# Three real products for a complex mix, an exact softshrink, and row swaps by SBUF transfers, in a Fourier mixer fused with a feed-forward block

## The chip, the cores and the metric

One core of a Trainium2 chip runs the whole program. The metric is the device time of one execution in microseconds (us); runs of one kernel mostly agree within 0.3%, and a kernel counts as faster or slower when its ratio to the one before differs from 1 by over 2%. Engines: TensorE (PE; its weight loads are PEld), VectorE (DVE), ScalarE (ACT), GpSimd (POOL), and SyncE (SP), which issues most transfers.

## The reference, cut to what matters

```python
# attention part: x is (8, 3008, 256)
X = np.fft.rfft(x, axis=1);  Xr, Xi = X.real, X.imag
Yr = Xr @ w_r - Xi @ w_i + b_r
Yi = Xr @ w_i + Xi @ w_r + b_i
Y  = softshrink(Yr, 0.01) + 1j * softshrink(Yi, 0.01)   # sign(y) * max(|y| - 0.01, 0)
y  = np.fft.irfft(Y, n=3008, axis=1)
# feed-forward part on the 24064 rows of y
h = np.maximum(y @ w_in, 0);  out = (s * h * h + b) @ w_out    # 256 -> 2048 -> 256
```

The feed-forward part is most of the arithmetic. The Fourier transform of length 3008 = 94 x 32 is done as matrix products: a first DFT over 94, a second over 32 (with twiddles), the complex mix with w_r and w_i, the inverse over 32, and the last DFT over 94.

## The kernel before: the parts concerned

The program interleaves two streams on TensorE. "Tiles" of the feed-forward block are cut in slots (one slot: two matmuls of the first layer and four or so of the second). Into chosen slots it puts small "units" of the transform of later batches: the second DFT, mix and inverse of batch b run while the feed-forward block works on batch b-1. Batch 0 has its own code at the start.

```python
def fwd_unit(i):                     # second DFT, two row groups
    ...                              # 4 matmuls -> one PSUM bank
    xt = xfpool.tile([P, 2 * DC, 192], F16)
    evac(xt[:, :, 64:192], ps, 512)                     # ACT or DVE, by a load balance
    nc.vector.tensor_scalar_mul(out=xt[:, :, 0:64], in0=xt[:, :, 128:192], scalar1=-1.0)

def mix_unit(i):                     # Xr w_r - Xi w_i and Xr w_i + Xi w_r
    for j in range(2):
        for m, (w, lo) in enumerate(((0, 64), (1, 0))):
            for dc in range(DC):
                matmul(ps[:, j, :], xt[:, j * DC + dc, lo : lo + P], W_t[:, dc, w], ...)   # 8 in all
    nc.vector.tensor_tensor(out=m, in0=ps, in1=lamb, op=max)
    nc.vector.scalar_tensor_tensor(out=z, in0=ps, scalar=2 * LAM, in1=m, op0=add, op1=min)

def inv_unit(i): ...                 # 2 matmuls with z, one copy to v, stored to DRAM
def s4_unit(g):                      # last DFT
    nc.vector.scalar_tensor_tensor(out=yt[...], in0=off, scalar=bl, in1=ps, op0=mult, op1=add)
```

The two DVE ops of the mix give the softshrink up to a constant offset, and the last DFT takes the offset's transform off again. All units share two PSUM banks (`psf`). In the views, `psh` and `psa` are the PSUM tiles of the feed-forward block's two layers, `rt` and `gt` its SBUF tiles; `u` goes to DRAM as `ud` and comes back as `us`, and `v` likewise. Line numbers (L557) differ from kernel to kernel.

## Time and profile before

| | before |
|---|---|
| time, median (4 runs) | 884.32 us (884.15 to 887.18) |
| span in the profile | 881.7 us, mean granted TensorE clock 0.999 |
| busy: PE, DVE, ACT, POOL | 97%, 75%, 71%, 3% |
| mix | 672 matmuls of 256 columns |
| transfers by the SP queue | 76,802 packets, 70 MB, 26.8% of the 16 engines' span |

The prediction below shows the lines and how they are read. The point to keep is that a matmul's listed duration is its depth in the pipe; the start-to-start distance is the pace.

### The profile page before, as it was taken

The numbers are of one execution on the slowest core, as the hardware profiler recorded it, in microseconds if no ns is written. First come the engines' busy times: TensorE is split into PE (matmuls) and PEld (weight loads), VectorE is DVE, ScalarE is ACT, GpSimd is POOL, SyncE is SP. The second block draws the span as 40 slices with busy tenths as digits, with TensorE's granted clock in tenths as the row PEclk, the third lists the DMA queues.
The fourth block names the chain that finished last, engine by engine and source line by source line (L and its number), as shares of the span: only waits on it lengthen the run. The fifth ranks groups of instructions, "written<-read, shape, count | busy, mean of one in ns | idle before, by whom it ended". The sixth has DMA issues, their size and how long they took to land.

```text
span 881.7 us, 16393 instructions
## 1 busy us (share of the span) xinstructions
PE 856.1 (97%) x6748; PEld 613.9 (70%) x6748; DVE 659.5 (75%) x846; ACT 621.9 (71%) x779; POOL 27.7 (3%) x51
## 2 busy tenths in 40 slices
PE   4989999999999999999999999999999999999997
PEld 3856776777767766777667776777767777766665
DVE  6797778677787778777787777787777767876663
ACT  4786776766777776777777777777767776676663
POOL 4010000000000000000000000000000000000000
PEclk9999999999999999999999999999999999999999
DMA  8764156313462237412563236712254111411111
GB/s 176 131 188 123 57 123 170 116 48 73 128 176 87 60 96 177 134 49 64 135 160 95 62 83 145 185 48 61 61 161 115 48 50 49 125 37 36 36 38 54
DMA packets 83021, 87.29 MB, mean 99 GB/s; under 512 B 5502, under 2 KB 75266, under 8 KB 81474
## 3 DMA queue, kind: packets, MB, share of 16 engines
q1 hardware_dynamic: 76802, 70.25, 26.8%
q0 software_dynamic: 6144, 15.99, 10.6%
q8 instruction: 53, 0.87, 0.4%
q14 instruction: 22, 0.18, 0.1%
HBM read 53.98 MB, written 46.66 MB: 114 GB/s over the span
## 4 chain that ended last, share of the span: by engine, by line
PE 83%; DVE 5%; ACT 5%; DMA 4%; issue 2%; SPq 0%; POOL 0%; DVEq 0%; ACTq 0%; POOLq 0%
PE psa L750 33%; PE psh L681 33%; PE psf L557 8%; PE psf L507 2%; PE psf L623 2%; ACT rt L688 2%; PE psf L539 2%; PE psf L575 2%; DVE gt L695 2%; DMA x<-in_x_dram 1%; DMA vs<-vd 1%; DMA ud<-u 1%; ACT u L172 1%; DVE g L376 1%; DVE yt L628 0%
## 5 line engine op out<-in xcount | busy, mean ns | idle before, releaser
L688 ACT ACTIVATE rt<-psh 128x1024 f32<-128x1024 f32 (+2 forms) x384 | 386.3, 1007 | 175.5 <-PE psh L681 174.2
L695 DVE TENSOR_TENSOR gt<-rt 128x1024 f16<-128x1024 f32 (+2 forms) x300 | 361.8, 1208 | 136.3 <-ACT rt L688 133.3
L750 PE MATMUL psa<-w_out_t,gt 128*128 128x256 f16 (+1 forms) x3024 | 457.1, 272 | 0.1
L750 PEld LDWEIGHTS <-gt 128*128 128x128 f16 (+1 forms) x3024 | 300.1, 101 | 181.6 <-issue 1.4
L681 PE MATMUL psh<-yt,w_in 128*128 128x512 f16 (+1 forms) x1344 | 397.9, 378 | 0.0
L681 PEld LDWEIGHTS <-w_in 128*128 128x128 f16 x1536 | 144.6, 98 | 25.1 <-issue 1.2
L760 DVE SCALAR_TENSOR_TENSOR ost<-psa,s_bc,bias_bc 128x512 f32<-128x512 f32 (+1 forms) x96 | 70.9, 739 | 23.5 <-PE psa L750 21.1
L557 PE MATMUL psf<-W_t,xf 128*128 128x256 f16 x672 | 87.1, 273 | 0.3 <-DVE xf L176 0.3
L692 ACT ACTIVATE gt<-rt 128x1024 f16<-128x1024 f32 (+2 forms) x84 | 85.7, 1020 | 2.0
L557 PEld LDWEIGHTS <-xf 128*128 128x128 f16 x672 | 65.7, 98 | 8.2 <-issue 0.7
L172 ACT CAST u<-psf 96x512 f16<-96x512 f32 x93 | 53.9, 581 | 23.5 <-PE psf L507 23.5
L628 DVE SCALAR_TENSOR_TENSOR yt<-off,bl,psf 128x480 f16<-128x480 f32 (+1 forms) x98 | 61.9, 666 | 7.6 <-PE psf L623 6.5
L565 DVE SCALAR_TENSOR_TENSOR z<-psf,m 128x512 f16<-128x512 f32 x84 | 58.1, 692 | 2.9
L563 DVE TENSOR_TENSOR m<-psf,lamb 128x512 f32<-128x512 f32 x84 | 57.5, 685 | 2.7 <-PE psf L557 2.5
L172 ACT CAST v<-psf 128x512 f16<-128x512 f32 x82 | 47.6, 580 | 17.0 <-PE psf L575 17.0
L172 ACT CAST xf<-psf 128x512 f16<-128x512 f32 x79 | 46.1, 584 | 10.5 <-PE psf L539 10.5
L681 PE MATMUL psh<-tail,w_in 128*128 128x512 f16 (+1 forms) x192 | 53.4, 353 | 0.0
L507 PE MATMUL psf<-x,A_t 94*96 94x512 f16 x104 | 39.9, 383 | 1.4 <-DVE z L565 0.5
L623 PEld LDWEIGHTS <-vs 96*128 96x128 f16 x448 | 28.9, 97 | 10.3 <-issue 4.1
L623 PE MATMUL psf<-C_t,vs 96*128 96x96 f16 x448 | 33.6, 205 | 0.8 <-ACT u L172 0.3
L539 PE MATMUL psf<-F_t,us 128*128 128x128 f16 x336 | 32.5, 219 | 1.5 <-DMA us<-ud 1.3
L196 POOL DMA_DIRECT2D x<-in_x_dram x32 | 17.0, 533 | 499.8 <-PE psf L507 464.6
(73 smaller groups left out, 312.5 us busy)
## 6 DMA issues: line engine op xcount, KB each, us to landing
out_dram<-ost SPq DMA_DIRECT2D x152, 128.0 KB
x<-in_x_dram POOLq DMA_DIRECT2D x32, 376.0 KB, 6.6
ud<-u SPq DMA_DIRECT2D x28, 384.0 KB
us<-ud SPq DMA_DIRECT2D x28, 384.0 KB
vd<-v SPq DMA_DIRECT2D x42, 256.0 KB
vs<-vd SPq DMA_DIRECT2D x14, 768.0 KB
out_dram<-ost SPq DMA_DIRECT2D x16, 120.0 KB
off<-offset_signal POOLq DMA_DIRECT2D x1, 1536.0 KB, 9.7
```

The source lines that it names most:

```text
L172: return None, nc.scalar.copy(out=dst, in_=src)
L507: nc.tensor.matmul(ps[0:96, :], A_t[0:N1, :], x16[(b, c)][0:N1, j * D : (j + 2) * D], start=True, stop=True,)
L557: nc.tensor.matmul(ps[:, j, :], xt[:, j * DC + dc, lo : lo + P], W_t[:, dc, w], start=(m == 0 and dc == 0), stop=(m == 1 and dc == DC - 1),)
L565: nc.vector.scalar_tensor_tensor(out=z, in0=ps, scalar=2 * LAM, in1=m, op0=ALU.add, op1=ALU.min)
L623: nc.tensor.matmul(ps[:, j * 96 : (j + 1) * 96], vs[(b, h)][:, k, ec * P : (ec + 1) * P], C_t, start=True, stop=True,)
L628: nc.vector.scalar_tensor_tensor(out=yt[:, ec, n2 : n2 + w, :], in0=off[0][:, n2 : n2 + w, :], scalar=bl[:, 1, ec : ec + 1], in1=ps[:, 0 : ...
L681: nc.tensor.matmul(o, w_in_t[dc][:, mc * P : (mc + 1) * P], r, start=(dc == 0), stop=(dc == DC - 1),)
L688: nc.scalar.activation(out=rt[:, :, 0:w], in_=ps[:, :, 0:w], func=AF.Relu)
L692: nc.scalar.activation(out=gt[:, :, 0:w], in_=rt[:, :, 0:w], func=AF.Square)
L695: nc.vector.tensor_tensor(out=gt[:, :, 0:w], in0=rt[:, :, 0:w], in1=rt[:, :, 0:w], op=ALU.mult)
L750: nc.tensor.matmul(ps[0:size, h, :], gts[(ti, mc // 2)][:, mc % 2, sub * size : (sub + 1) * size], w_out_t[:, mc, :], start=(mc == 0), sto ...
L760: nc.vector.scalar_tensor_tensor(out=ost[0:size, 0:k], in0=ps[0:size, 0:k], scalar=s_bc[0:size], in1=bias_bc[0:size, 0:k], op0=ALU.mult, o ...
```

## The change

Its intent: with S = (Xr + Xi) w_r, one has Yr = S - Xi (w_i + w_r) and Yi = S + Xr (w_i - w_r), so three real products do the work of four. The softshrink becomes exact (y - clamp(y, -0.01, 0.01)), done on fp16 sums in SBUF, so the offset at the last DFT goes. The price is a layout: results come out with two row groups and two parts (real, imaginary) crossed, and four 32 KB SBUF to SBUF transfers per unit (the swaps) put the rows where the inverse DFT wants them. The tiles `t`, `m` and `z` of the mix lie in one SBUF buffer, called `ring` in the views, so a swap is `ring<-ring`.

```diff
 def fwd_unit(i):
-    evac(xt[:, :, 64:192], ...)
-    nc.vector.tensor_scalar_mul(out=xt[:, :, 0:64], in0=xt[:, :, 128:192], scalar1=-1.0)
+    evac(xt[:, 1:3], bank, 512)
+    nc.vector.tensor_tensor(out=xt[:, 0], in0=xt[:, 1], in1=xt[:, 2], op=ALU.add)   # Xr + Xi
+def sum_unit(h):                              # one for two mix units: 4 matmuls
+    ... matmul(ps[:, i, :], xf[2 * h + i][:, 0, dc], W_t[:, dc, 0], ...)
+    nc.scalar.copy(out=s, in_=ps)
 def mix_unit(i):
-    ... 8 matmuls; max; add-and-min from PSUM
+    ... 4 matmuls with W_g
+    nc.vector.tensor_tensor(out=t, in0=ps, in1=s, op=ALU.add)       # PSUM -> fp16 ring
+    nc.vector.tensor_tensor(out=m, in0=t, in1=low, op=ALU.max)
+    nc.vector.tensor_tensor(out=m, in0=m, in1=high, op=ALU.min)
+    nc.vector.tensor_tensor(out=t, in0=t, in1=m, op=ALU.subtract)
+    for j in range(2):
+        for r in range(2):
+            nc.sync.dma_start(out=z[64*r : 64*r+64, j], in_=t[64*j : 64*j+64, r])
...
+    # inverse units follow their mix by four units; two empty units before the last four
 def s4_unit(g):
-    nc.vector.scalar_tensor_tensor(out=yt[...], in0=off, scalar=bl, in1=ps, ...)
+    evac(yt[...], ps, w * 96)                                       # ACT or DVE
...
+    make_w_g(); make_bounds()      # five POOL ops while batch 0 is mixed
```

More of the change, by code (lines that the diff above doesn't have):

```diff
@@ L70, in _tables @@
     return first, fwd, inv, last
-def _offset_signal(inv, last):
-    v = inv.reshape(2, 2, N2, NPAIR, 2, N2).sum(axis=2)
-    v = v.transpose(0, 2, 1, 3, 4).reshape(2, 96, N2)
-    return np.einsum("rkn,km->rnm", v, last)
 def _tile_order(nb):
@@ L130 @@
     T_d = nc.inline_tensor(inv.astype(np.float16), name="dft_inv").ap()
-    off_r, off_i = _offset_signal(inv, last)
-    IMPULSE = float(off_r[0, 0])
-    off_r[0, 0] = 0.0
-    assert np.abs(off_r[:, :N1]).max() < 1e-9
-    G_d = nc.inline_tensor(off_i.astype(np.float32).reshape(1, -1), name="offset_signal").ap()
     C_d = nc.inline_tensor(last.astype(np.float16), name="dft_last").ap()
@@ L152 @@
     uspool = ctx.enter_context(tc.tile_pool(name="usp", bufs=5))
-    xfpool = ctx.enter_context(tc.tile_pool(name="xfp", bufs=3))
+    xfpool = ctx.enter_context(tc.tile_pool(name="xfp", bufs=4))
     mpool = ctx.enter_context(tc.tile_pool(name="mp", bufs=2))
-    zpool = ctx.enter_context(tc.tile_pool(name="zp", bufs=3))
     vpool = ctx.enter_context(tc.tile_pool(name="vp", bufs=3))
@@ L232 @@
     nc.sync.dma_start(out=C_t, in_=C_d)
-    b_one = cpool.tile([P, D], F32, name="b_one")
+    b_st = rpool.tile([P, 2, D], F32, name="b_st", tag="rt")
     for i, bv in enumerate((b_r, b_i)):
-        nc.sync.dma_start(
-            out=b_one[64 * i : 64 * i + 64], in_=bv.unsqueeze(0).to_broadcast([64, D])
-        )
-    lamb = cpool.tile([P, 2, D], F32, name="lamb")
-    bl = cpool.tile([P, 2, DC], F32, name="bl")
-    for i, bv in enumerate((b_r, b_i)):
-        nc.sync.dma_start(out=bl[:, i], in_=bv.rearrange("(c p) -> p c", p=P))
+        nc.sync.dma_start(out=b_st[:, i], in_=bv.unsqueeze(0).to_broadcast([P, D]))
+    low = cpool.tile([P, 2, D], F16, name="low")
+    high = cpool.tile([P, 2, D], F16, name="high")
+    W_g = cpool.tile([P, DC, 2, D], F16, name="W_g")
     s_bc = cpool.tile([P, 1], F32, name="s_bc")
@@ L270, with make_bounds, make_w_g @@
         nc.vector.memset(f, 0.0)
-    def make_lamb():
-        for j in range(2):
-            nc.vector.tensor_scalar(
-                out=lamb[:, j], in0=b_one, scalar1=-1.0, scalar2=LAM, op0=ALU.mult, op1=ALU.add
-            )
+    def make_bounds():
+        for t, c in ((low, -LAM), (high, LAM)):
+            nc.gpsimd.tensor_scalar(
+                out=t, in0=b_st, scalar1=-1.0, scalar2=c, op0=ALU.mult, op1=ALU.add
+            )
+    def make_w_g():
+        nc.gpsimd.tensor_tensor(out=W_g[:, :, 1], in0=w_st[1], in1=w_st[0], op=ALU.subtract)
+        nc.gpsimd.tensor_tensor(out=W_g[:, :, 0], in0=w_st[1], in1=w_st[0], op=ALU.add)
+        nc.gpsimd.tensor_scalar_mul(out=W_g[:, :, 0], in0=W_g[:, :, 0], scalar1=-1.0)
     def blocks(t):
@@ L315 @@
     vs = {}
+    ring = []
     yts = {}
@@ L402, in fwd_dft @@
             nc.scalar.activation(out=pos, in_=ps, func=AF.Relu, bias=neg_lam)
-            z = zpool.tile([P, 4, P], F16, name="z", tag="z")
+            z = gpool.tile([P, 4, P], F16, name="z", tag="gt")
             nc.vector.scalar_tensor_tensor(
@@ L480, in first_batch @@
             if i == 6:
-                with tc.issue_after(g_last[0].ins):
-                    make_lamb()
-                nc.gpsimd.tensor_scalar_add(out=bl[:, 1], in0=bl[:, 1], scalar1=-LAM)
-                nc.gpsimd.tensor_scalar(
-                    out=bl[:, 0], in0=bl[:, 0], scalar1=-LAM, scalar2=IMPULSE,
-                    op0=ALU.add, op1=ALU.mult,
-                )
+                make_w_g()
+                make_bounds()
         for k in range(4):
@@ L528, in s23_units @@
         vd = dpool.tile([NPAIR, P, D], F16, name="vd", tag="vd")
+        if not ring:
+            ring.append(bigpool.tile([P, 12, 2, D], F16, name="ring", tag="corr"))
         xf = {}
@@ L533, in fwd_unit @@
         def fwd_unit(i):
-            ps = one_bank().rearrange("p (j c k) -> p j c k", j=2, c=DC)
+            bank = one_bank()
+            ps = bank.rearrange("p (r c j k) -> p r c j k", r=2, c=DC, j=2)
             t = us[(b, i // 3)]
@@ L539, in fwd_unit @@
                     nc.tensor.matmul(
-                        ps[:, j, dc, :], t[:, q, dc * P : (dc + 1) * P],
+                        ps[:, :, dc, j, :], t[:, q, dc * P : (dc + 1) * P],
                         F_t[:, 2 * i + j, :], start=True, stop=True,
                     )
-            xt = xfpool.tile([P, 2 * DC, 192], F16, name="xf", tag="xf")
-            evac(xt[:, :, 64:192], ps.rearrange("p j c k -> p (j c) k"), 512)
-            nc.vector.tensor_scalar_mul(
-                out=xt[:, :, 0:64], in0=xt[:, :, 128:192], scalar1=-1.0
-            )
@@ L548, in fwd_unit @@
-            load["dve"] += 0.2
-            xf[i] = xt
-        def mix_unit(i):
-            ps = one_bank().rearrange("p (j e) -> p j e", j=2)
-            xt = xf.pop(i)
-            for j in range(2):
-                for m, (w, lo) in enumerate(((0, 64), (1, 0))):
-                    for dc in range(DC):
-                        nc.tensor.matmul(
-                            ps[:, j, :], xt[:, j * DC + dc, lo : lo + P], W_t[:, dc, w],
-                            start=(m == 0 and dc == 0), stop=(m == 1 and dc == DC - 1),
-                        )
-            m = mpool.tile([P, 2, D], F32, name="m", tag="m")
-            nc.vector.tensor_tensor(out=m, in0=ps, in1=lamb, op=ALU.max)
-            z = zpool.tile([P, 2, D], F16, name="z", tag="z")
-            nc.vector.scalar_tensor_tensor(
-                out=z, in0=ps, scalar=2 * LAM, in1=m, op0=ALU.add, op1=ALU.min
-            )
-            load["dve"] += 1.38
+            xt = xfpool.tile([P, 3, DC, P], F16, name="xf", tag="xf")
@@ new lines, in fwd_unit @@
+            evac(xt[:, 1:3].rearrange("p r c k -> p (r c k)"), bank, 512)
+            nc.vector.tensor_tensor(out=xt[:, 0], in0=xt[:, 1], in1=xt[:, 2], op=ALU.add)
+            load["dve"] += 0.25
+            xf[i] = xt
+        def sum_unit(h):
+            ps = one_bank().rearrange("p (i e) -> p i e", i=2)
+            for i in range(2):
+                for dc in range(DC):
+                    nc.tensor.matmul(
+                        ps[:, i, :], xf[2 * h + i][:, 0, dc], W_t[:, dc, 0],
+                        start=(dc == 0), stop=(dc == DC - 1),
+                    )
+            s = mpool.tile([P, 2, D], F32, name="s", tag="m")
+            nc.scalar.copy(out=s, in_=ps)
+            load["act"] += 0.6
+            hold[h] = s
@@ new lines, in mix_unit @@
+        def mix_unit(i):
+            ps = one_bank().rearrange("p (r e) -> p r e", r=2)
+            xt = xf.pop(i)
+            for r in range(2):
+                for dc in range(DC):
+                    nc.tensor.matmul(
+                        ps[:, r, :], xt[:, 2 - r, dc], W_g[:, dc, r],
+                        start=(dc == 0), stop=(dc == DC - 1),
+                    )
+            t, m = ring[0][:, i % 4], ring[0][:, 4 + i % 2]
+            nc.vector.tensor_tensor(
+                out=t, in0=ps, in1=hold[i // 2][:, i % 2].unsqueeze(1).to_broadcast([P, 2, D]),
+                op=ALU.add,
+            )
+            nc.vector.tensor_tensor(out=m, in0=t, in1=low, op=ALU.max)
+            nc.vector.tensor_tensor(out=m, in0=m, in1=high, op=ALU.min)
+            nc.vector.tensor_tensor(out=t, in0=t, in1=m, op=ALU.subtract)
+            load["dve"] += 1.75
+            z = ring[0][:, 6 + i % 6]
+            for j in range(2):
+                for r in range(2):
+                    nc.sync.dma_start(
+                        out=z[64 * r : 64 * r + 64, j], in_=t[64 * j : 64 * j + 64, r]
+                    )
@@ L597, in s23_units, with put @@
         units = []
-        for i in range(H + 2):
-            if i < H:
-                units.append(lambda i=i: fwd_unit(i))
-            if 0 <= i - 1 < H:
-                units.append(lambda i=i: mix_unit(i - 1))
-            if 0 <= i - 2 < H:
-                units.append(lambda i=i: inv_unit(i - 2))
+        def put(f, i, n):
+            if 0 <= i < n:
+                units.append(lambda: f(i))
+        for h in range(H // 2 + 3):
+            for i in range(2):
+                put(fwd_unit, 2 * h + i, H)
+                put(mix_unit, 2 * h - 2 + i, H)
+                put(inv_unit, 2 * h - 6 + i, H)
+            put(sum_unit, h, H // 2)
+            if h == H // 2:
+                units += [lambda: None] * 2
         return units
@@ L627, in unit @@
                 )
-            nc.vector.scalar_tensor_tensor(
-                out=yt[:, ec, n2 : n2 + w, :], in0=off[0][:, n2 : n2 + w, :],
-                scalar=bl[:, 1, ec : ec + 1],
-                in1=ps[:, 0 : w * 96].rearrange("p (j n) -> p j n", n=96),
-                op0=ALU.mult, op1=ALU.add,
-            )
-            load["dve"] += 0.15 + w / 10.0
-            if n2 == 0:
-                nc.vector.tensor_scalar_add(
-                    out=yt[:, ec, 0, 0:1], in0=yt[:, ec, 0, 0:1], scalar1=bl[:, 0, ec : ec + 1]
-                )
+            evac(
+                yt[:, ec, n2 : n2 + w, :],
+                ps[:, 0 : w * 96].rearrange("p (j n) -> p j n", n=96), w * 96,
+            )
             if g == len(groups) - 1 and b >= 2:
@@ L778 @@
     load.update(act=0.0, dve=0.0)
-    off = []
-    def emit_load_off():
-        off.append(bigpool.tile([P, N2, 96], F32, name="off", tag="corr"))
-        nc.gpsimd.dma_start(
-            out=off[0].rearrange("p n m -> p (n m)"), in_=G_d.to_broadcast([P, N2 * 96])
-        )
     mark = {}
@@ L793 @@
     plan.setdefault(17, []).append(lambda: emit_load_x(2))
-    plan.setdefault(30, []).append(emit_load_off)
     schedule(22, 44, s23_units(1))
```

## The prediction

> **What bounds the kernel now.** I read the page's busy table first, then its slices, then the time-ordered view of one stretch, then the waits and windows.
>
> ```profile
> PE 856.1 (97%) x6748; PEld 613.9 (70%) x6748; DVE 659.5 (75%) x846; ACT 621.9 (71%) x779; POOL 27.7 (3%) x51
> ...
> PE   4989999999999999999999999999999999999997
> ```
>
> TensorE is busy from the second slice to the last; VectorE (DVE) and ScalarE (ACT) have about a quarter free. But matmuls are pipelined, so "busy" may hide slack. The test is the pace, from the time-ordered view around 181 us:
>
> ```profile
> 181.56 1.04 PE L557 MATMUL psf<-W_t,xf 128*128 128x256 f16 x8
> 181.56 0.22 DVE L545 TENSOR_SCALAR xf<-xf 128x256 f16<-128x256 f16 x1
> 182.33 0.21 PEld L681 LDWEIGHTS <-w_in 128*128 128x128 f16 x2
> 182.38 1.23 DVE L695 TENSOR_TENSOR gt<-rt 128x1024 f16<-128x1024 f32 x1 [0.60 <-ACT rt L688]
> 182.43 0.59 PE L681 MATMUL psh<-yt,w_in 128*128 128x512 f16 x2
> ```
>
> The reader is to see the two PE starts: eight mix matmuls begin at 181.56 and the next matmul at 182.43, so eight take 0.87 us, 109 ns each, though the group row gives each a duration of 273 ns (its depth in the pipe). 256 columns at the page's full clock cannot go much faster. The windows view says that this holds all through the steady part:
>
> ```profile
> 165.00:205.00 40.00, 40.00 (x313) 29.99 (x312) 28.95 (x39) 28.52 (x36) 0.00 (x0) 1.00 0.16 47
> ```
>
> Columns: PE, weight loads, DVE, ACT and POOL busy in 40 us. PE never pauses; DVE is at 72%, ACT at 71%. The waits view charges PE only a few tenths of a us here and there after 64 us. The chain of work that ended last is 83% PE. So the bound is the stream of matmul columns; only about 15 us at the start and 12 us after the last first-layer matmul are anything else.
>
> **What the Trainium skill says.** "TensorE: Matmul & The Clock Gate", Back-to-back issue gap: 262 cycles for N=256 warm, which is 109 ns; the trace's 0.87/8 agrees exactly. "Perfetto Trace Analysis", Identifying the Most-Contended Engine, says matmul busy share is a poor measure and weight-load busy share a better one; here that share is only 70% while the pace is at its floor, so for this mix of shapes I trust the pace. "VectorE: DVE Perf Modes", The perf-mode tier table with the errata section: a two-input op runs 1x with fp32 or PSUM and 2x with 16-bit SBUF operands, and a fp32 one takes (N+151)/0.96 ns. The trace agrees for 1x: L695 with N=1024 has 1223 ns against 1224. No two-input 16-bit op is in this trace, so the 2x cost is an estimate from that page. "DMA: Bandwidth & Descriptors", Anatomy of one DMA: about 2 us fixed for a transfer, mostly the confirmation that it landed. No small SBUF copy is in this trace; the nearest thing is a 3.2 us us<-ud step in the chain of waits.
>
> **The change part by part.** The rows concerned:
>
> ```profile
> L557 PE MATMUL psf<-W_t,xf 128*128 128x256 f16 x672 | 87.1, 273 | 0.3 <-DVE xf L176 0.3
> L565 DVE SCALAR_TENSOR_TENSOR z<-psf,m 128x512 f16<-128x512 f32 x84 | 58.1, 692 | 2.9
> L563 DVE TENSOR_TENSOR m<-psf,lamb 128x512 f32<-128x512 f32 x84 | 57.5, 685 | 2.7 <-PE psf L557 2.5
> L628 DVE SCALAR_TENSOR_TENSOR yt<-off,bl,psf 128x480 f16<-128x480 f32 x84 | 56.3, 708 | 4.1 <-PE psf L623 3.2
> L545 DVE TENSOR_SCALAR xf<-xf 128x256 f16<-128x256 f16 x84 | 18.4, 222 | 17.6 <-ACT xf L172 17.4
> ```
>
> *TensorE.* Eight mix matmuls per unit become four, plus four for each two units: 672 go to 336 + 168 = 504. 168 fewer at 109 ns is **18.3 us**. Every one lies on the path that sets the end, so with nothing else changed 884.2 - 18.3 = 865.9 us, 2.1% less. All other matmuls keep their shape; the built program's instruction list confirms the counts.
>
> *VectorE.* Per mix unit, before: 0.222 + 0.685 + 0.692 = 1.60 us, times 84 = 134 us. After: the sum of two halves, 256 fp16 (estimate (128+151)/0.96 = 0.29 us); the add from PSUM (0.685, like L563); max, min and subtract on 512 fp16 (estimate (256+151)/0.96 = 0.42 each). That is 2.25 us, times 84 = 189 us: +55 us. The last-DFT evacuations lose the offset term: 62 us at L628 and 3 us of one-column fixes leave; by the built order 31 of the 98 plain copies stay on DVE (about 19 us), 67 go to ACT. The kernel's load balancer also moves 22 squares (23 us) and some 18 copies (12 us) to DVE. Sum: 659.5 + 55 - 65 + 19 + 23 + 12 = **704 us**, 81% of 866.
>
> *ScalarE.* 42 new copies of the shared product (0.58 us each, like the other L172 rows: 24 us), 67 copies from the last DFT (35 us), less 22 squares (20 us) and 18 copies (10 us): **651 us**, 75%.
>
> *Transfers.* 336 row swaps of 64 x 512 B, 32 KB each, 11 MB in all; one 1.5 MB offset load goes. The DMA share is 0.16 in the window above, so bandwidth is ample. The SP queue that issues them spends 0.37 us on a vd<-v issue and 0.57 on an output row block, so four swaps are an estimated 1.5 to 2.4 us of SP time per mix unit, which comes every 5 to 6 us. A swapped tile is now an input of the inverse DFT, but that is emitted four mix units later, some 15 to 20 us, against about 2 us of DVE chain, 2 us of issue and 2 to 3 us of landing: hidden. Only the last two units of a batch have shorter leads, about 8 us. The reshaped forward output (two runs of 64 columns) costs no columns.
>
> *Start.* The bounds and the combined weights are made on POOL while the first batch runs; POOL is 3% busy. Neutral within a us.
>
> **The rivals.** (1) *The saving is whole*: PE is at its floor and everything new hides, 866 us. For it: DVE and ACT stay under saturation on average, and 15 gt buffers let DVE lag. Against it: averages. (2) *DVE becomes the near-bound in the mix stretches.* Mix units fill only 44 to 66 of each 80 to 96 first-layer slots. Placing the durations above by slot in the built order, DVE work rises from about 0.77 to 0.89-0.97 of PE's own time there (0.98 in the densest, batch 1's 44 slots), ACT from 0.77 to 0.87; some of that is overlap between neighbours, so call it 0.85-0.94. All small matmul groups share two PSUM banks; a bank waits for its evacuation behind a 2 us DVE chain or a 1.2 us square, while units follow every 1.2 to 1.7 us. That makes short PE stalls: I put 0.05 to 0.15 us per mix unit, 4 to 12 us over 84, most in batch 1 and batch 3. Working for it: PSUM is freed after one DVE op (0.69 us) instead of two (1.38). Time 870 to 878. (3) *The swaps take the place of the removed matmuls as a wait*: SP issues in order and reuses its completion slots, so a slow 768 KB load or an output waiting for its producer would hold swaps back, and PE with them. Each batch's last units could lose 1 us: 873 or so; a lead that is too short everywhere would cost a us per unit, 950, but the four-unit lag speaks against it. (4) *Relief for the last-DFT stretch*, where DVE was fullest: worth nothing, since PE had no gaps there.
>
> **Range and chances.** 865.9 plus about 6 us of stalls: **872 us**. Low end 865 (no stalls, a us off the start), high end 884 (DVE stalls of 18 us, the gain gone). Faster by over 2% needs 866.8 or less, that is under 1 us of new stalls: 0.14. Slower by over 2% needs 36 us of stalls: 0.06. Within 2%: 0.80.
>
> **What would show it.** PE rows for the mix: 504 matmuls, 109 ns apart. DVE near 700 us, its fp16 rows near 0.42 us, 0.29 for the sum. In the windows of the mix stretches, PE short of the full stretch by a few per cent, its waits naming the ring add, the xf sum or an ACT copy (rival 2), or the ring's DMA (rival 3). It would be wrong if the 16-bit ops run at 1x (0.69 us each: +67 us of DVE, saturated, no gain or a loss), if the swaps land later than 10 us, or if PE shows no new waits at all (then 866).

## More of the kernel before

The next batch's x comes in four pieces of 376 KB, issued from POOL; each piece is fetched as soon as the first DFT has consumed the piece whose buffer it takes.

## The result

The changed kernel took 874.86 us (median of 4 runs, 873.02 to 878.13) against 884.32: ratio 0.989 with a 95% interval of 0.9852 to 0.9927. Ratios here are the mean time of one kernel's runs over that of the other's runs of the same rounds, so not quite the ratio of the medians. By the 2% rule it is "same": 1.1% faster, where the matmul count alone promised 2.1%. Its runs spread more, and with the clock: 873.0 and 873.9 us had a mean granted clock of 0.994, 875.8 and 878.1 had 0.989.

The page of the changed kernel, in the same places as the lines of before: the busy table, the PE slices, and the groups of the new mix (count, then busy us and mean ns, then idle time of the engine ahead of the group and what ended it).

```profile
PE 838.8 (96%) x6580; PEld 599.4 (69%) x6580; DVE 693.4 (80%) x971; ACT 640.7 (74%) x848; POOL 32.8 (4%) x53
...
PE   4889999999899999999999999999999999999996
...
L563 DVE TENSOR_TENSOR ring<-psf,s 128x512 f16<-128x512 f32 x84 | 57.4, 683 | 3.4 <-PE psf L558 3.3
...
L558 PE MATMUL psf<-W_g,xf 128*128 128x256 f16 x336 | 50.4, 273 | 0.0
...
L585 PE MATMUL psf<-ring,T_t 128*128 128x256 f16 x168 | 33.2, 275 | 7.7 <-DMA ring<-ring 7.6
L569 DVE TENSOR_TENSOR ring<-ring,high 128x512 f16<-128x512 f16 x84 | 35.5, 422 | 2.1
L570 DVE TENSOR_TENSOR ring<-ring 128x512 f16<-128x512 f16 x84 | 35.4, 422 | 2.0
```

The new DVE ops cost what was estimated (422 ns), DVE is 34 us busier, and one figure has no counterpart before: L585, the inverse DFT, kept PE idle for 7.6 us, waiting for the ring's transfers. The windows view says where PE still runs without a gap and where not (same columns as in the prediction; the last three are granted clock, share of the transfer engines, GB/s):

```profile
165.00:205.00 40.00, 40.00 (x313) 29.99 (x312) 33.83 (x58) 31.38 (x41) 0.00 (x0) 1.00 0.24 68
...
225.00:245.00 20.00, 16.80 (x104) 10.93 (x103) 11.88 (x15) 11.72 (x16) 0.51 (x1) 0.91 0.62 152
```

In the middle of a batch's mixes DVE is busy 85% of the time and PE 100%. At the end of the batch PE loses 3.2 us of 20, DVE is less busy than elsewhere (59%), the transfer engines are at 62%, and the clock is 0.91. The kernel before had the transfer engines as full in the same 20 us (0.61), but no swap to wait for:

```profile
225.00:245.00 20.00, 19.95 (x139) 13.79 (x137) 14.58 (x17) 14.43 (x20) 1.03 (x2) 1.00 0.61 149
```

In the changed kernel the chain of waits, in time order, names the link:

```profile
227.65 0.45 PE psh L689 x2
228.10 0.05 SPq L576
228.15 0.05 issue
228.20 7.72 DMA ring<-ring
235.92 0.14 issue
236.05 0.27 PE psf L585
```

A 32 KB swap issued at 228.2 lands at 235.9. The time-ordered view around it:

```profile
227.62 3.34 SPq L576 DMA_DIRECT2D ring<-ring  x4
...
227.95 0.51 POOL L182 DMA_DIRECT2D x<-in_x_dram  x1 [12.75 <-PE psf L493]
...
236.05 0.63 PE L585 MATMUL psf<-ring,T_t 128*128 128x256 f16 x2 [3.18 <-DMA ring<-ring]
236.48 1.06 PE L689 MATMUL psh<-yt,w_in 128*128 128x512 f16 x2
237.33 1.06 PE L758 MATMUL psa<-w_out_t,gt 128*128 128x256 f16 x4
```

Two things stand here. A piece of the next x was issued at 227.95, between the swaps. In the trace's packet records its 94 packets of 4 KB, which began between 230.0 and 235.1, held their engines for 482 ns each on the mean (median 324), where the 512-byte packets of these 9 us, the swaps' among them, took 29 ns. And after the pause PE is slow: two matmuls of 512 columns from 236.48 to 237.33 are 0.85 us, 426 ns each, in place of 216. The clock records show a stretch of 3.41 us at half clock from 236.4; another begins at 127.2, after a wait of 2.1 us that ends at 126.4. All the PE waits for the ring (2.1, 3.2, 1.2, 0.3 and 0.8 us at the ends of batches 1 to 5) have an x piece issued 1 to 8 us ahead; batches 6 and 7, which have no further x to load at that point, have none.

The start differs as well. In the time-ordered view, VectorE's four copies into `T_t`, before and after:

```profile
19.17 2.27 DVE L301 COPY T_t<-T_c 32x1536 f16<-32x1536 f16 x4
```

```profile
18.47 4.65 DVE L291 COPY T_t<-T_c 32x1536 f16<-32x1536 f16 x4
...
20.33 1.49 POOL L265 TENSOR_TENSOR W_g<-w_st 128x512 f16<-128x512 f32 x1
21.81 0.90 POOL L257 TENSOR_SCALAR low<-b_st 128x512 f16<-128x512 f32 x1
22.69 1.78 POOL L266 TENSOR_SCALAR W_g<-W_g 128x512 f16<-128x512 f16 x1
```

They take twice as long beside the new POOL ops, and the waits view of the changed kernel has a PE wait of 2.2 us for the first DVE result `g` there.

So the theory is: the saving on PE is whole; it is reduced by (A) swaps at the end of a batch that land late because a piece of x uses the same transfer engines (A1), the two longest pauses followed by half clock, and (C) POOL and DVE blocking each other at the start. The rivals: the lead of the last swaps is too short in any case (A2), or DVE at 80% is what costs (B).

### The profile page after: what moved, and what is told of

Its sections match the earlier page's. It is cut to its first block, busy times and chain, and to the rows that moved or that the text cites. A ratio compares the mean times of both kernels' runs of the same rounds, so it can differ in the third digit from the quotient of the medians.

```text
span 871.1 us, 16955 instructions
## 1 busy us (share of the span) xinstructions
PE 838.8 (96%) x6580; PEld 599.4 (69%) x6580; DVE 693.4 (80%) x971; ACT 640.7 (74%) x848; POOL 32.8 (4%) x53
## 4 chain that ended last, share of the span: by engine, by line
PE 89%; DMA 5%; ACT 2%; DVE 2%; issue 1%; SPq 1%; POOL 0%; DVEq 0%; POOLq 0%
PE psh L689 36%; PE psa L758 36%; PE psf L558 4%; DMA ring<-ring 3%; PE psf L493 3%; PE psf L529 2%; PE psf L544 2%; PE psf L638 2%; PE psf L585 2%; DMA x<-in_x_dram 1%; ACT rt L696 1%; DVE T_t L291 1%; PE psh L357 1%; ACT yt L158 0%; ACT m L393 0%
## 5 line engine op out<-in xcount | busy, mean ns | idle before, releaser
L703 DVE TENSOR_TENSOR gt<-rt 128x1024 f16<-128x1024 f32 (+2 forms) x322 | 385.8, 1200 | 111.2 <-ACT rt L696 110.7
L700 ACT ACTIVATE gt<-rt 128x1024 f16<-128x1024 f32 (+2 forms) x62 | 65.4, 1055 | 0.9
L563 DVE TENSOR_TENSOR ring<-psf,s 128x512 f16<-128x512 f32 x84 | 57.4, 683 | 3.4 <-PE psf L558 3.3
L558 PE MATMUL psf<-W_g,xf 128*128 128x256 f16 x336 | 50.4, 273 | 0.0
L158 ACT CAST yt<-psf 128x480 f16<-128x480 f32 (+2 forms) x71 | 36.4, 526 | 10.8 <-PE psf L638 10.7
L585 PE MATMUL psf<-ring,T_t 128*128 128x256 f16 x168 | 33.2, 275 | 7.7 <-DMA ring<-ring 7.6
L569 DVE TENSOR_TENSOR ring<-ring,high 128x512 f16<-128x512 f16 x84 | 35.5, 422 | 2.1
L570 DVE TENSOR_TENSOR ring<-ring 128x512 f16<-128x512 f16 x84 | 35.4, 422 | 2.0
L568 DVE TENSOR_TENSOR ring<-ring,low 128x512 f16<-128x512 f16 x84 | 35.3, 420 | 1.5
L558 PEld LDWEIGHTS <-xf 128*128 128x128 f16 x336 | 32.9, 98 | 3.7
L182 POOL DMA_DIRECT2D x<-in_x_dram x32 | 16.7, 525 | 492.3 <-PE psf L493 456.0
```

The source lines that it names most:

```text
L158: return None, nc.scalar.copy(out=dst, in_=src)
L558: nc.tensor.matmul(ps[:, r, :], xt[:, 2 - r, dc], W_g[:, dc, r], start=(dc == 0), stop=(dc == DC - 1),)
L563: nc.vector.tensor_tensor(out=t, in0=ps, in1=hold[i // 2][:, i % 2].unsqueeze(1).to_broadcast([P, 2, D]), op=ALU.add,)
L569: nc.vector.tensor_tensor(out=m, in0=m, in1=high, op=ALU.min)
L585: nc.tensor.matmul(ps[:, j, :], T_t[:, 2 * i + j, :], z[:, j, :], start=True, stop=True)
L700: nc.scalar.activation(out=gt[:, :, 0:w], in_=rt[:, :, 0:w], func=AF.Square)
```

## The experiments

Runs of one call share a chip and its runs of the kernel before (883.68, 883.83, 884.01 and 884.15 us in the four calls). Differences in us are taken from the ratios, times 884.

**1. The changed kernel again**, as the base on this chip.

> The changed kernel again, as the base for the runs beside it. Its first four runs spread from 873.0 to 878.1 us with granted clocks of 0.994 and 0.989. All theories: 873 to 878, ratio to before about 0.989. If pauses of TensorE that halve its clock are the cause of the spread, its slower runs have the lower mean clock (about 0.002 for each half-clock stretch of 3.4 us).

873.0 us (869.0 to 875.5), ratio 0.9877 (0.9856 to 0.9898), clocks 0.992 to 0.995; its slowest runs do not have the lowest clocks here, so the tie of spread and clock is loose. Its trace has the same waits at the same places (8.0 us for the ring) and half-clock stretches at 52.6, 127.7 and 236.9 us.

**2. No swaps** (wrong result).

```diff
-nc.vector.tensor_tensor(out=t, in0=t, in1=m, op=ALU.subtract)
+nc.vector.tensor_tensor(out=z, in0=t, in1=m, op=ALU.subtract)     # z = ring[0][:, 6 + i % 6]
-... four nc.sync.dma_start(...) per unit
```

> The last op of the softshrink writes straight into the inverse DFT's input and the 336 row swaps are gone (wrong result on purpose; DVE, ACT and PE work unchanged). Theory A (the lost part of the gain is PE waiting for the last swaps of a batch, and the half clock that follows): 7.6 us of waits and about 3 us of half clock go, less what takes their place: 864 to 867, clock 0.998. Rival B (VectorE as near-bound): no change, 873 to 878.

862.45 us, ratio 0.9754 (0.9741 to 0.9767): 10.9 us less than the base, a little more than theory A asked for. DVE did the same work (695 us busy), so rival B falls for this part. The forecast clock of 0.998 did not come: the runs had 0.993 to 0.997, and the profile has 6.8 us of half clock from 23.7 us, at the start, around a PE wait of 4.1 us for the first `g`. After the start it has none.

**3. The loads of x held back** past the swaps of the batch.

```diff
+def gated_load_x(b):
+    gate = nc.gpsimd.tensor_copy(out=gate_t[0:1, 0:1], in_=newest[0][0:1, 0, 0:1])  # newest gt tile
+    with tc.issue_after(gate.ins):
+        emit_load_x(b)
-plan.setdefault(s1 + 6, []).append(lambda b=b: emit_load_x(b + 1))
+plan.setdefault(s1 + 6, []).append(lambda b=b: gated_load_x(b + 1))
```

> Same kernel, but the loads of the next batch's x (376 KB pieces) are held back on POOL until six first-layer slots into the next batch, so that none runs beside the last swaps of a batch. Theory A1 (the swaps land late because a piece of x shares the transfer engines: all six PE waits come within 1 to 8 us of an x issue): waits of L585 for the ring nearly vanish, 865 to 868. Rival A2 (the lead is too short anyway, or SP issues too slowly): little change, 871 to 877. Rival B: no change.

863.68 us, ratio 0.9771 (0.9758 to 0.9783), correct: 9.4 us less than the base and a little below A1's forecast, with every swap still there. In the time-ordered view of POOL, the pieces that had come one by one now come together, well ahead of the batch's end:

```profile
167.45 0.18 POOL L679 COPY gate_t<-gt 1x1 f16<-1x1 f16 x1 [103.27 <-DVE gt L710]
167.94 2.05 POOL L182 DMA_DIRECT2D x<-in_x_dram  x4 [0.30 <-PE psf L558]
```

and of PE's waits for the ring one is left, in batch 3, with its landing in the chain of waits:

```profile
318.94 0.12 SPq L576
319.06 0.05 issue
319.11 1.83 DMA ring<-ring
320.94 0.05 issue
320.99 0.28 PE psf L585
```

A swap lands in 1.8 us where no piece of x runs beside it. The changed kernel says the same by itself: in its chain of waits, the two swaps with no piece of x issued in the 8 us before land in 2.0 us (at 115.8) and 1.8 us (at 314.1), the five others in 4.4 to 7.7. So A1 is shown: not the swap's own cost, but what it met.

**4. More lead** (rival A2).

```diff
-units += [lambda: None] * 2
+units += [lambda: None] * 6
```

> Six empty units in place of two ahead of the last four inverse DFTs of a batch, in the same span: 3 to 6 us more lead for the last swaps, the other units packed a little closer. Theory A (late swaps): 866 to 870. Rival B (VectorE): the denser packing makes it worse, 876 to 882.

874.37 us, ratio 0.9898 (0.9881 to 0.9914): no gain, so theory A's forecast for this run was wrong. The trace shows part of why. Lead did grow in batches 2 and 4 to 7 (from 5 to 9 us between the last softshrink's end and its inverse DFT to 11.5 to 12), and the waits of batches 2, 4 and 5 went. But in batch 1, which has 44 slots for now 48 units, DVE finished the last softshrink 5.2 us after its matmuls began, the swaps were issued at 125.0 behind other entries of the SP queue, a piece of x at 124.6 ran beside them, and one landed after 6.4 us: PE waited 3.5 us there, more than before, with a half-clock stretch after it. This profile also had a longer wait at the start (4.4 us against 2.2) and 6.8 us of half clock there. PE's waits for the ring still fell in sum, from 7.6 to 4.2 us. That the closer packing spent what the lead gained is argued from batch 1 alone and not shown. Nor does the run speak for rival A2, because the edit also moved the swaps relative to the loads. In batches 2, 4 and 5 the last softshrink now ended 7.0 to 7.4 us ahead of the next piece of x (1.2 to 1.6 in the changed kernel), and the waits went; in batches 1 and 3 it ended 2.0 and 3.8 us ahead, and a wait stayed.

**5. The POOL ops held back** until the `T_t` copies are done.

```diff
+gate2 = nc.gpsimd.tensor_copy(out=w_gate[96:97, 0:1], in_=T_t[96:97, 0, 64:65])
+with tc.issue_after(gate2.ins):
     make_w_g(); make_bounds()
```

> The changed kernel with one edit: the five POOL ops that make the combined weights and the bounds wait until VectorE's copies into T_t are done. In the traces of the changed kernel these copies (three in 1.7 us before) take 4.1 us beside the POOL ops, and TensorE then waits 2.2 to 4.4 us for the first DVE g. Theory C (POOL and DVE block each other there, and in some runs a half-clock stretch follows): PE's wait for the first g falls under 0.5 us and the time by 2 to 5 us, to 868 to 871. Rival (harmless, or other transfers are the cause): 871 to 875.

870.23 us, ratio 0.9842 (0.9821 to 0.9863): 3.1 us less than the base, give or take 2.6 by the two intervals; experiment 6 against 3 gives 3.3, give or take 1.7. Theory C's gain holds, and the copies are back at their old cost:

```profile
18.91 2.25 DVE L292 COPY T_t<-T_c 32x1536 f16<-32x1536 f16 x4
```

Which POOL work slowed them is less clear. The second copy of the changed kernel (19.03 to 20.70) ran mostly beside the issue of a load of w_out (19.14 to 20.33), before the first POOL op shown above, and in this run that issue came at 17.1. The edit moved both and does not separate them.

**6. Both edits.**

> Both edits, the held-back loads of x and the held-back POOL ops. If the two losses are independent they add: 863.7 less 2 to 5, so 859 to 862, mean clock 0.998 as before. If the POOL effect is nothing: 863.7.

860.57 us, ratio 0.9734 (0.972 to 0.9749), correct, and the fastest valid version here: the two gains add (9.4 + 3.1 from 0.9877 would be 0.9736). Three of its four runs have the clock 0.998 of the kernel before.

**7. Only the matmuls gone, in the kernel before** (wrong result): two of each unit's eight left out.

```diff
-for dc in range(DC):
+for dc in range(DC - m):
```

> The kernel BEFORE with two of each unit's eight mix matmuls left out (168 in all; wrong result on purpose), nothing else changed. It measures what the removed matmuls alone are worth. Theory (TensorE's pace is the bound): 168 x 109 ns = 18.3 us, so 865 to 866. Rival (part is lost to new waits on DVE even with no added DVE work): 868 to 875.

866.25 us, ratio 0.9793 (0.9775 to 0.9811): 18.3 us (16.7 to 19.9), the sum of 168 x 109 ns.

**8. The matmuls put back, in the version with both edits** (wrong result): the shared product's four matmuls twice.

```diff
-for dc in range(DC):
+for k in range(2 * DC):
+    dc = k % DC
```

> The version with both edits, with the shared product's four matmuls done twice (168 more, back to 672; wrong result on purpose). Theory (TensorE's pace is the bound after as well): both-edits time plus 18.3 us, 877 to 880. If VectorE or the transfers were the bound after the change: less, plus 5 to 12.

877.7 us, ratio 0.9924 (0.9906 to 0.9941): 16.8 us more than without them. PE's pace is the bound after the change as before it. The 1.5 us short of 18.3 are within the two intervals.

**9. Less DVE work, in the version with both edits** (wrong softshrink; the comparison still passed, so its tolerance does not tell the two apart).

```diff
-tensor_tensor(out=m, in0=t, in1=low, op=max); tensor_tensor(out=m, in0=m, in1=high, op=min)
-tensor_tensor(out=t, in0=t, in1=m, op=subtract)
+tensor_tensor(out=t, in0=t, in1=low, op=subtract)
```

> The version with both edits, with max, min and subtract of the softshrink replaced by one subtract (wrong result on purpose): 168 VectorE ops of 0.42 us fewer, 71 us of its 694, and the swaps start 0.9 us earlier. If VectorE's load (prediction's main rival, 4 to 12 us of stalls) still costs TensorE anything, the time falls from 860.6 by 3 us or more. If VectorE is hidden: within 1 us, 859.6 to 861.5.

859.01 us, ratio 0.9709 (0.9695 to 0.9722), 2.2 us less by the ratios: between the two forecasts. The windows view of the middle of a batch, for the version with both edits and for this one:

```profile
165.00:205.00 40.00, 40.00 (x313) 29.57 (x311) 34.65 (x59) 31.69 (x43) 1.22 (x3) 1.00 0.48 111
```

```profile
165.00:205.00 40.00, 40.00 (x314) 29.70 (x313) 28.52 (x44) 31.14 (x41) 1.77 (x4) 1.00 0.48 107
```

DVE fell from 87% to 71% of these 40 us and PE was full in both. PE's distance from its floor, summed over start-to-start times, differs in the middle of the program only in batch 3 (2.5 us against 1.0 between 260 and 345 us), where the last wait for a swap has gone. So these DVE ops cost about 2 us in all, and the 1.5 us of it that the trace shows went into the start of that swap, not into evacuations.

**10 and 11. What else the change gained, and a control.** The version with both edits is 5.2 us faster than experiment 7 (0.9734 against 0.9793), with the same matmul count. In the kernel before, PE's weight loads (PEld) had small waits, of which these are the largest after the start, in the waits view from 64 us on (us in total, times, longest; "issue" means that the profile shows nothing that was waited for):

```profile
PEld L623 <- issue: 4.1, 16, 0.3
PEld L507 <- DVE z L565: 3.3, 6, 0.7
```

L623 is the last DFT, L507 the first DFT behind a mix. Experiment 10 gives the kernel before the change's plain evacuation of the last DFT:

```diff
-nc.vector.scalar_tensor_tensor(out=yt[...], in0=off, scalar=bl, in1=ps, op0=mult, op1=add)
+evac(yt[...], ps, w * 96)
```

> The kernel BEFORE with the last DFT evacuated by plain copies shared between ScalarE and VectorE, as the change does (the offset is not added: wrong result on purpose). The version with both edits is 5.7 us faster than the kernel before less 168 matmuls, so the rest of the change gains something. If it is this evacuation (TensorE waits 16 times, 4.1 us, at the last DFT's weight loads in the kernel before): 879 to 882. If it is the earlier release of the mix banks: 883 to 884.

882.57 us, ratio 0.9979 (0.9966 to 0.9991): 1.9 us, between the two forecasts. The L623 row has shrunk from 4.1 us to 0.6:

```profile
PEld L623 <- issue: 0.6, 3, 0.2
```

Experiment 11 holds the x loads back in the kernel before, with the edit of experiment 3:

> Control: the kernel BEFORE with its x loads held back in the same way. If holding them back is worth something by itself, 878 to 882; if it only takes them out of the way of the new swaps, as theory A1 says, 883 to 885.

883.45 us, ratio 0.9993 (0.998 to 1.0006): nothing, as A1 says.

**12. Mix banks free after one DVE op**, on top of experiment 10 (wrong result).

```diff
-nc.vector.scalar_tensor_tensor(out=z, in0=ps, scalar=2 * LAM, in1=m, op0=add, op1=min)
+nc.vector.scalar_tensor_tensor(out=z, in0=m,  scalar=2 * LAM, in1=m, op0=add, op1=min)
```

> The kernel BEFORE with the plain last-DFT evacuation (as in the run before, 0.998 of before) and, besides, its second mix op reading the first op's SBUF result in place of PSUM, so that a mix bank is free after one VectorE op of 0.69 us and not two (1.38 us), with the same count of ops (wrong result on purpose). If holding the mix banks costs TensorE its small waits (3.3 us at the first DFT's weight loads for z, and others): a further 1.5 to 3 us off, 879.5 to 881, ratio 0.995 to 0.9965. If not: as the run before, 882 to 883.

879.94 us, ratio 0.995 (0.9936 to 0.9965): a further 2.6 us with equal DVE time (57.5 and 58.1 us in the two groups, as before); the row of L507 waiting for z is gone. (The two runs are of different calls, so the 2.6 us has an uncertainty of 1.7.) The two together are 4.4 of the 5.2 us. The rest, under 1 us, is within the intervals and stays open. One candidate that no run tests: PE waits once, near 73 us, for `us<-ud` in the kernel before (1.3 us) and in experiment 7 (1.6), and not in the version with both edits.

## Why the prediction was right, and which steps were not

The measured 874.86 us lies 2.9 us from the predicted 872 and inside the range of 865 to 884; "within 2%" was right. Step by step:

- **The saving of 18.3 us is whole**, within the noise. Experiment 7 measured 18.3, experiment 8 16.8, each give or take about 2.
- **The costs of the engines were well sized.** DVE 693 us (predicted 704), ACT 641 (651), the fp16 ops 422 ns (0.42 us) and 284 ns (0.29), four swaps 2.4 us of SP time (1.5 to 2.4), a median of 15 us from the softshrink's end to the inverse DFT (15 to 20).
- **Rival 2, "I put 0.05 to 0.15 us per mix unit, 4 to 12 us over 84", was the wrong term.** Its stalls are the only ones that the prediction's range names. PE was at 100% with DVE at 85%; the waits that were to be its sign came to 0.4 us for the xf sum and none for the ring add; and experiment 9 found about 2 us behind DVE, mostly the start of one swap. Its counterweight, "PSUM is freed after one DVE op", was named but not sized: experiment 12 shows 2.6 us of gain for it, in the kernel before. So the sign was wrong: on balance the DVE side of the change helped PE.
- **Rival 3 was the cause, in the place named but under-sized.** "Each batch's last units could lose 1 us" were 0.3 to 3.2 us in five batches, 7.6 in sum, plus half-clock stretches; taken together 9.4 us (experiment 3). The landing of "2 to 3 us" holds only in a quiet stretch (1.8); beside a piece of x it was 4.4 to 7.7. The statement that "bandwidth is ample", from a DMA share of 0.16, was read in a window in the middle of a batch; at its end the share was 0.61 in the very trace that the prediction read.
- **"Neutral within a us" at the start was wrong**: 3.1 us (experiment 5). The 3% busy share of POOL says nothing of what a POOL op blocks.
- **Rival 4, relief of the last DFT "worth nothing, since PE had no gaps there", was wrong by 1.9 us** (experiment 10). Its weight loads had sixteen waits of at most 0.3 us there, too small to be seen in a busy share. The waits view had them (4.1 us for L623, 3.3 for L507); the prediction's "a few tenths of a us here and there" read the matmul rows and passed over those of the weight loads.

In ratios, from the base of 1: 0.0207 saved by the matmuls (experiment 7), 0.0059 that the version with both edits gains beyond that (0.0050 of it shown by experiments 10 and 12), 0.0106 lost to the late swaps, 0.0035 lost at the start; that leaves 0.9875, and experiment 1 measured 0.9877. This is no separate test: the 0.0059 is itself a remainder, so the sum only repeats that the two losses add. Predicted losses of 6 us met a real loss of 12.5 and a gain of 5.2. The net of these, 7.3, lies near 6 by luck: two errors cancelled.

## What to carry to other kernels

When a change adds small transfers with a deadline, ask at the place of the deadline, not on average, which large transfers run there and what triggers them; moving the large one (here a load with much time to spare) was worth 9.4 us, half of what the saved arithmetic was worth. When an engine runs at its floor, look for waits in the waits view rather than in busy shares: sixteen waits of at most 0.3 us are invisible in the one and plain in the other, if the rows of the weight loads are read too. Setup work on an idle engine need not be free: here it cost 3.1 us through copies on another.

## What the Trainium skill lacked or had wrong

- "TensorE: Matmul & The Clock Gate", Part 1 puts the loss of the full clock at an idle window of about 3.4 us. Here waits of 2.1 and 3.2 us in the changed kernel, 1.9 and 2.2 in its second run, 2.2 in experiment 12 and 3.5 in experiment 4 were each followed by 3.41 us at half clock (512 columns in 426 ns), while waits of 1.2 and 1.8 us (changed kernel, second run) and of 1.5 us (experiment 5) were not. The length of the stretch agrees with the page's window; the pause that suffices is shorter than its rule of thumb. A long pause is not needed either: the stretches at 52.6 us (second run), 53.2 (experiment 3) and 50.9 (experiment 10) have only PE waits of 0.3 to 0.65 us in the 5 us before them; what set them off stays open.
- "SBUF — State Buffer", Who interferes with whom, says that two-port VectorE copies and GpSimd ops block each other. The trace agrees and gives a size: four copies of 32x1536 fp16 took 4.65 us beside POOL's setup work and 2.27 and 2.25 without it (experiment 5 says what is not separated there).
- "DMA: Bandwidth & Descriptors", Anatomy of one DMA, has about 2 us fixed, under a heading for transfers issued by POOL. A 32 KB SBUF to SBUF swap issued by SP agrees alone (1.83 us to landing), but the page has no figure for a small transfer beside a large one: 4.4 to 7.7 us beside a 376 KB load, whose 4 KB packets took 482 ns on the mean in the slowest case.
- "Perfetto Trace Analysis", Identifying the Most-Contended Engine, recommends weight-load share, beside MFU (not worked out here), for TensorE's headroom: it was 70% and 69% in kernels whose matmuls started at their floor of 109 ns for 256 columns, and 168 matmuls fewer were worth their full 18.3 us.
